# Two heads' low parts of P in one GpSimd operation, and another table for the sums ahead of the main loop

## The chip, the cores and the metric

The kernel runs on one core of a Trainium2 chip. The metric is the time in microseconds that the device takes for one launch; smaller is better. The kernel before takes 1578.27 us, the median of three runs (1576.91 to 1578.88).

## What is computed

Attention over a band of 256 keys and a bilinear feed-forward network share one normalised input; the network's output gates the attention's.

```
H = 32; Dh = D // H; W = 256                      # B, S, D, F = 1, 2048, 576, 4608
xn = layernorm(x)
q, k, v = split(xn @ wqkv)                         # per head, 18 wide
scores = einsum("bhqd,bhkd->bhqk", q, k) * Dh**-0.5
p = softmax(where(0 <= q_index - k_index < W, scores, -1e9))
s = (p @ v) @ wo
g = silu(((xn @ w_gate) * (xn @ w_up)) @ w_down)
out = x + s * g
```

## The kernel before

Every matrix product works on 16-bit floats, and each operand is split in two parts, a high and a low one (the value rounded to 16 bits, and what the rounding left), so that a product is hi*hi + hi*lo + lo*hi.

The program has a prologue and a main loop. The prologue (lines 660 to 855) normalises x into `XT`, projects V, Q and K, and writes them to memory in the device. The main loop (lines 1287 to 1291) has 72 slots of 16 places: slot `sl` is the feed-forward network's step for group `g = sl // 4` of 256 hidden columns and chunk `c = sl % 4` of 512 rows. TensorE's work of a place is issued by `seven_place` (lines 1150 to 1180), a fast matrix product with seven products of blocks instead of eight. It needs sums of blocks of x (`SX`, from `s_steps`, lines 525 to 592, made once for each chunk) and of the weights (`TW`, from `t_sum`, `t_hi`, `t_lo`, lines 494 to 519, made anew for each group). `seven_read` reads the products out of the PSUM banks named `up`, of which there are two: a product that writes into a bank waits until ScalarE (`seven_copy`, L1126) or VectorE (`seven_add`, L1130) has read it. `seven_mult` (L1135) multiplies, once on GpSimd (`ht`) and once on VectorE (in place in `gt`). `h_hi` (L1002, ScalarE) and `h_lo` (L1008, VectorE) split the result into `hh`, and `down` (L1024) multiplies it by the third weight.

Everything else hangs on a list of times: `at(slot, place, f, ...)` queues a call, `at_place` issues the calls of a place, and the dict `AT` holds the numbers. The engines run their own instructions strictly in the order in which these calls issue them, so that AT is the order of the work on each engine.

Attention has 64 steps, one in each of the slots 1 to 64. A step `s` takes a pair of heads `j = 0, 1` for four blocks `i = 0..3` of 128 queries. For each of the eight (i, j) five calls follow one another at places of the table "p": `score` (L908, VectorE, writes the masked scores to a tile `sm_` and their maximum), `shifted` (L916), `probs` (L920, the exponential on ScalarE; with j = 1 also L923, which rounds both heads' P to the high parts in the tile `pp`), `turn_probs` (L929, the low parts: P minus its high part, into the same `pp`; with j = 1 also L932, the transposing DMA from `pp` to `pt`) and `weigh` (L941, the product with V). Both heads of an i share one tile `sm_` of 2 x 384 floats, and there are two such tiles (line 905), so block i + 2 writes where block i was read. The steps 0 to 15 have shorter rows (128, 256, 384, 384 keys for i = 0..3); later ones have 384 each.

The line that decides who makes the low parts is L929 in `turn_probs`: `AT["en"][(s + 1) % 4][2 + 2 * i + j]` is 0 for GpSimd and 1 for VectorE. All four rows of "en" are (0, 1, 0, 0, 0, 0, 1, 0, 0, 0): for i = 0, 1, 3 both heads are GpSimd's, for i = 2 the first head is VectorE's and the second GpSimd's.

The prologue's part of the order is in the entries "sx" (time of each of the 17 steps of `s_steps` for each chunk), "on" (which of these are VectorE's, 1, or GpSimd's, 0), and "g0", "t0", "u0", "wd0" (group 0's weights).

Of the kernel before, what the change touches and what calls it, by code (L numbers as in the profile page):

```python
# [13 lines left out]
OP = mybir.AluOpType  # L14
# [6 lines left out]
def kernel(  # L21
# [10 lines left out]
    nc = tc.nc  # L32
# [6 lines left out]
    NCH = S // 512  # L39
# [28 lines left out]
    AT = {"amax": (19, 20, 6),  # L68
           "dn": ((41, 45), (51, 52), (52, 48)),
           "down": ((6, 9, 12, 15, 20), (6, 8, 11, 14, 16), (6, 8, 11, 14, 16), (6, 9, 12, 15, 19)),  # L70
           "en": ((0, 1, 0, 0, 0, 0, 1, 0, 0, 0), (0, 1, 0, 0, 0, 0, 1, 0, 0, 0),
                  (0, 1, 0, 0, 0, 0, 1, 0, 0, 0), (0, 1, 0, 0, 0, 0, 1, 0, 0, 0)),
           "end": ((30, 32, 35), (28, 32, 33), (28, 32, 33), (28, 32, 33)),
           "eng": (1, 1, 0, 1, 1, 0, 1, 0, 0, 0, 0, 0, 0, 1),
           "g0": (-22, -19, -22, -21, -9, -16, -14, -11, -11),
           "h": (((15, 17), (18, 21)), ((15, 17), (19, 21)), ((15, 17), (21, 21)), ((15, 17), (19, 21))),
           "load": (8, 3, 15),
           "mult": {1: 6, 4: 18, 5: 1, 6: 0},
# [13 lines left out]
           "raw": (8, 9, 12, 16, -6, 0),  # L92
           "scale": (26, 28, 35, 51),
           "sum": ((30, 36, 50, 59, 64), (41, 53, 56, 61, 62)),
# [5 lines left out]
           "t_hi": ((57, 57), (67, 69)),  # L100
           "t_lo": ((57, 58), (70, 71)),
           "u0": ((-9, -8, -7, -7), (-7, -7, -7, -4)),
           "up_hi": (36, 36, 60, 61),
           "up_lo": (41, 40, 65, 62),
           "wd": ((55, 56), (65, 69), (70, 74)),
           "wd0": ((-4, 3), (-1, 4), (-1, 7))}

    ctx.enter_context(tc.manual_schedule())
    const = ctx.enter_context(tc.tile_pool(name="const", bufs=1))
# [573 lines left out]
    a, b = TB.pop(0)  # L683
# [96 lines left out]
    for t in range(16):  # L780
# [18 lines left out]
        elif t in (3, 5):  # L799

            k = (t + 5) // 2 - 1
# [54 lines left out]
    post = ctx.enter_context(tc.tile_pool(name="post", bufs=1, reuse_waits="tile"))  # L856
    acc = post.tile([128, NT, D], F32, name="acc")
    att = att_stack.enter_context(tc.tile_pool(name="att", bufs=1))
    QS, KS, VT, SP, SM, PP, PT, PVB, OB, O3, MX, SMT, RC = {}, {}, {}, {}, {}, {}, {}, {}, {}, {}, {}, {}, {}

    def unit(u, part, n0, n1):
        return qk_d[part:part + 3, u * DH:(u + 1) * DH, n0:n1]
# [55 lines left out]
    def probs(s, j, i):  # L918
        sm, mx, n = SM[s, j, i]
        nc.scalar.activation(sm, sm, AF.Exp, bias=mx[:, 1:2], scale=sig[:, 0:1])  # L920
        if j == 1:
            PP[s, i] = att.tile([128, 1536], F16, name="pp", bufs=3)
            nc.scalar.copy(PP[s, i][:, 0:2 * n].rearrange("p (j n) -> p j n", j=2), SMT.pop((s, i))[:, :, 384 - n:])  # L923


    def turn_probs(s, j, i):
        sm, mx, n = SM.pop((s, j, i))
        pp, a = PP[s, i], n * j
        (nc.gpsimd, nc.vector)[AT["en"][(s + 1) % NCH][2 + 2 * i + j]].tensor_tensor(pp[:, a + 2 * n:a + 3 * n], sm, pp[:, a:a + n], op=OP.subtract)  # L929
        if j == 1:  # L930
            pt = PT[s, i] = att.tile([128, 12, 128], F16, name="pt", bufs=3)
            nc.sync.dma_start(pt[:, 0:4 * n // 128], PP.pop((s, i))[:, 0:4 * n], transpose=True)  # L932
# [51 lines left out]
    for s in range(NSTEP):  # L984
        b = first_slot + s
        for f, p in zip((load_k, load_q, load_v), AT["load"]):
            at(b - 1, p, f, s)
        for k in range(2):
            at(b, AT["pairs"][k], score_pairs, s, 2 * k)
        for n in range(8):  # L990
            i, j = divmod(n, 2)
            for f, p in zip((score, shifted, probs, turn_probs, weigh), AT["p"][b % NCH][n]):
                at(b, p, f, s, j, i)
        at(b, AT["end"][b % NCH][0], finish, s)
        at(b, AT["end"][b % NCH][1], finish2, s)
        if s % 2 == 1:
            for part in range(3 if s % 16 == 15 else 2):
                at(b, AT["end"][b % NCH][2] + 2 * part, store_o, s // 16, s % 16 // 2, part)
# [327 lines left out]
```

## Time and profile before

| | |
|---|---|
| runs | 1578.27 us median (1576.91 to 1578.88) |
| the profiled execution | 1577.54 us, span 1575.8 us |
| TensorE busy | 1555.8 us, 99% |
| VectorE busy | 1268.4 us, 80% |
| ScalarE busy | 1069.8 us, 68% |
| GpSimd busy | 850.8 us, 54%, 1066 instructions |
| granted TensorE clock | 1.0 of full speed throughout |

The span is the time from the first to the last instruction of the profiled execution; the execution's own time is 1.7 us longer. Busy is the time in which an engine executes something, waits in an instruction that has begun included.

### The profile page before, as it was taken

Reading aid. Unit: us, or ns where it says so; the run is one execution under the profiler, and the core shown is the slowest. Engines: PE = TensorE matmul, PEld = TensorE weight load, DVE = VectorE, ACT = ScalarE, POOL = GpSimd, SP = SyncE. Lnnn points to the kernel's source line nnn. Section 1 sums busy time; section 2 is a strip of 40 time slices with the busy share of each in tenths; the row PEclk is TensorE's granted clock in tenths of the full one; section 3 lists DMA queues with packets and bytes.
Section 4 is the critical chain, followed back from the end, with each engine's and each line's share of the span. In section 5 each row is a group of like instructions: output and inputs, shape, how many; then the busy total and the mean of one; then the engine's idle time right before and its main releaser. Section 6 shows DMA issues by size and latency. Waiting matters only on the chain.

```text
span 1575.8 us, 40062 instructions
## 1 busy us (share of the span) xinstructions
PE 1555.8 (99%) x15498; PEld 1106.1 (70%) x15498; DVE 1268.4 (80%) x2756; ACT 1069.8 (68%) x1854; POOL 850.8 (54%) x1066
## 2 busy tenths in 40 slices
PE   8999999999999999999999999999999999999999
PEld 5465577777777777777777777777777777777767
DVE  6537688888888988898989888888888888877654
ACT  6535477777777878777778777878778787752230
POOL 4116455656465757575766666566757575742100
PEclk9999999999999999999999999999999999999999
DMA  8683436555557676777777677767696877651338
GB/s 221 200 249 129 164 73 135 100 127 108 121 107 139 126 148 127 144 139 139 139 129 156 119 148 125 155 119 150 118 154 128 152 124 148 120 103 33 68 83 219
DMA packets 566575, 212.14 MB, mean 135 GB/s; under 512 B 504560, under 2 KB 544624, under 8 KB 566384
## 3 DMA queue, kind: packets, MB, share of 16 engines
q1 hardware_dynamic: 566384, 209.58, 64.3%
q8 instruction: 121, 1.98, 0.6%
q14 instruction: 70, 0.57, 0.1%
HBM read 76.63 MB, written 29.00 MB: 67 GB/s over the span
## 4 chain that ended last, share of the span: by engine, by line
PE 86%; DVE 6%; POOL 2%; DMA 2%; issue 1%; ACT 1%; SPq 0%; DVEq 0%; POOLq 0%; ACTq 0%
PE up L1160 41%; PE dn L1024 22%; PE pv L941 4%; PE s L387 4%; PE up L1113 3%; PE s L897 2%; PE s L1024 2%; PE s L1263 2%; PE up L1263 2%; PE up L387 1%; DVE hh L1008 1%; DMA pt<-pp 1%; PE s L338 1%; POOL pp L929 1%; DVE tw L193 1%
## 5 line engine op out<-in xcount | busy, mean ns | idle before, releaser
L1024 PE MATMUL dn<-dnw,hh 128*128 128x512 f16 (+1 forms) x3168 | 444.7, 286 | 1.1
L1160 PEld LDWEIGHTS <-tw 128*128 128x128 f16 x3456 | 319.2, 97 | 63.5 <-DVE tw L193 6.0
L1024 PEld LDWEIGHTS <-hh 128*128 128x128 f16 x3456 | 222.4, 98 | 169.2 <-issue 19.2
L1160 PEld LDWEIGHTS <-upw 128*128 128x128 f16 x3024 | 283.9, 98 | 64.5 <-issue 22.2
L1130 DVE SCALAR_TENSOR_TENSOR gt<-up,gt 128x512 f32<-128x512 f32 x360 | 247.6, 688 | 60.7 <-PE up L1113 40.1
L1031 DVE SCALAR_TENSOR_TENSOR acc<-dn,sc,acc 128x512 f32<-128x512 f32 x310 | 215.2, 694 | 99.1 <-PE dn L1024 99.1
L1160 PE MATMUL up<-XT,upw 128*128 128x256 f16 x2160 | 276.6, 273 | 0.0
L916 ACT ACTIVATE mx<-mx,sig 128x2 f32<-128x2 f32 x256 | 98.0, 383 | 212.7 <-DVE mx L908 212.7
L1160 PE MATMUL up<-XT,tw 128*128 128x256 f16 x1728 | 234.8, 272 | 3.4 <-DVE gt L1130 3.4
L1160 PE MATMUL up<-sx,tw 128*128 128x256 f16 x1728 | 224.7, 272 | 2.6 <-DVE tw L193 2.5
L1135 POOL TENSOR_TENSOR ht<-gt 128x512 f32<-128x512 f32 x72 | 92.1, 1279 | 93.1 <-DVE gt L1130 92.3
L941 PEld LDWEIGHTS <-pt 128*128 128x128 f16 x2880 | 109.7, 96 | 38.1 <-DMA pt<-pp 3.0
L941 PE MATMUL pv<-vt,pt 128*128 128x37 f16 x2880 | 112.9, 179 | 1.9 <-DMA pt<-pp 1.9
L1160 PE MATMUL up<-sx,upw 128*128 128x256 f16 x864 | 112.7, 273 | 0.0
L1126 ACT ACTIVATE gt<-up 128x512 f32<-128x512 f32 x144 | 83.6, 581 | 30.8 <-PE up L1160 17.3
L1002 ACT ACTIVATE hh<-ht 128x512 f16<-128x512 f32 x72 | 45.2, 627 | 67.4 <-POOL ht L1135 67.4
L507 POOL TENSOR_TENSOR tf<-raw 128x256 f32<-128x256 f32 x102 | 83.5, 818 | 0.1
L507 POOL TENSOR_TENSOR tf<-raw,tf 128x256 f32<-128x256 f32 x68 | 62.0, 913 | 21.7 <-DVE tw L193 21.7
L193 DVE SCALAR_TENSOR_TENSOR upw<-raw,sc,upw 128x640 f16<-128x640 f32 x72 | 71.7, 998 | 0.0
L315 ACT ACTIVATE upw<-raw 128x1280 bf16<-128x1280 f32 (+1 forms) x51 | 62.5, 1226 | 5.9 <-DMA raw<-in_B_w_up_dram 5.6
L193 DVE SCALAR_TENSOR_TENSOR tw<-tf,sc,tw 128x512 f16<-128x512 f32 x68 | 49.4, 749 | 14.5 <-ACT tw L190 13.7
L897 PE MATMUL s<-ks,qs 54*128 54x384 f16 (+2 forms) x512 | 60.2, 312 | 0.0
(1355 smaller groups left out, 2921.8 us busy)
## 6 DMA issues: line engine op xcount, KB each, us to landing
raw<-in_B_w_down_dram SPq DMA_DIRECT2D x36, 288.0 KB
qk_d<-qp SPq DMA_DIRECT2D x18, 512.0 KB
raw<-in_B_w_gate_dram SPq DMA_DIRECT2D x36, 256.0 KB
raw<-in_B_w_up_dram SPq DMA_DIRECT2D x36, 256.0 KB
ks<-qk_d SPq DMA_DIRECT2D x96, 81.0 KB
qs<-qk_d SPq DMA_DIRECT2D x128, 54.0 KB
vt<-v_d SPq DMA_DIRECT2D x48, 111.0 KB
qk_d<-qp SPq DMA_DIRECT2D x20, 256.0 KB
```

Of the source, the lines that this page charges most:

```text
L193: nc.vector.scalar_tensor_tensor(w, rv, s, h, op0=OP.mult, op1=OP.subtract)
L387: nc.tensor.matmul(ps, a, b, start=i == 0 and not opened, stop=i == 12 and opened)
L507: nc.gpsimd.tensor_tensor(t[:, to], x0, x1, op=OP.subtract)
L897: nc.tensor.matmul(ps[:, :hi_ - lo_], QS[s][r, i * 128:(i + 1) * 128], KS[s][r, lo_:hi_], start=True, stop=True)
L916: nc.scalar.activation(mx[:, 1], mx[:, 0], AF.Identity, bias=sig[:, 2:3], scale=sig[:, 1:2])
L941: nc.tensor.matmul(PVB[s][:, j, i, :VW], pt[:, nb * j + n + n // nb * nb], VT[s][:, lo_ + n % nb, j * VW:(j + 1) * VW], start=n == 0, stop ...
L1024: nc.tensor.matmul(to, a, b, start=q == 0, stop=q == len(l) - 1)
L1031: nc.vector.scalar_tensor_tensor(d, src, SC[g][:, 9:10], d, op0=OP.mult, op1=OP.add)
L1126: nc.scalar.activation(seven_new(sl, name), CH[q], AF.Copy, scale=H_SC)
L1130: nc.vector.scalar_tensor_tensor(seven_new(sl, name), CH[q], H_SC, x, op0=OP.mult, op1=OP.add)
L1135: eng.tensor_tensor(HT[sl, f], u[:, 0], u[:, 1], op=OP.mult)
L1160: nc.tensor.matmul(CH[q][:, o], a, b, start=CH["first"], stop=last and q not in (1, 2, 5), skip_group_check=q in ON)
```

## The change

`turn_probs` no longer issues two operations where both heads of a block are GpSimd's: the call with j = 0 issues nothing, and the call with j = 1 issues one operation over both heads (2 x n elements in a row, read from the whole tile `sm_`, which `probs` now keeps in `BOTH`). Where the heads are shared between the engines (i = 2) nothing changes. The lines after the function move down by eight.

```diff
         if j == 1:
             PP[s, i] = att.tile([128, 1536], F16, name="pp", bufs=3)
-            nc.scalar.copy(PP[s, i][:, 0:2 * n].rearrange("p (j n) -> p j n", j=2), SMT.pop((s, i))[:, :, 384 - n:])
+            nc.scalar.copy(PP[s, i][:, 0:2 * n].rearrange("p (j n) -> p j n", j=2), SMT[s, i][:, :, 384 - n:])
+            BOTH[s, i] = SMT.pop((s, i))
...
     def turn_probs(s, j, i):
         sm, mx, n = SM.pop((s, j, i))
         pp, a = PP[s, i], n * j
-        (nc.gpsimd, nc.vector)[AT["en"][(s + 1) % NCH][2 + 2 * i + j]].tensor_tensor(pp[:, a + 2 * n:a + 3 * n], sm, pp[:, a:a + n], op=OP.subtract)
+        on = AT["en"][(s + 1) % NCH][2 + 2 * i:4 + 2 * i]
+        e = (nc.gpsimd, nc.vector)[on[j]]
+        if on[0] != on[1]:
+            e.tensor_tensor(pp[:, a + 2 * n:a + 3 * n], sm, pp[:, a:a + n], op=OP.subtract)
+        elif j == 1:
+            h, l = (pp[:, 2 * n * k:2 * n * k + 2 * n].rearrange("p (j n) -> p j n", j=2) for k in range(2))
+            e.tensor_tensor(l, BOTH.pop((s, i))[:, :, 384 - n:], h, op=OP.subtract)
```

The table changes in the entries that set the prologue's order; the ones of the main loop ("p", "dn", "h", "sum", "t_hi" and so on) stay. Of it only two lines:

```diff
-           "g0": (-22, -19, -22, -21, -9, -16, -14, -11, -11),
+           "g0": (-22, -22, -20, -23, -10, -15, -14, -11, -11),
...
-           "wd0": ((-4, 3), (-1, 4), (-1, 7))}
+           "wd0": ((-4, 0), (-1, 6), (-1, 7))}
```

TensorE's order and that of the DMA queue (SP) stay as they were, instruction by instruction. GpSimd loses 192 of its 448 operations of L929, and one operation of the sums goes from it to VectorE.

GpSimd's order in the last of a group's four slots (c = 3), in the middle of the main loop, before. `sm__17215` holds block i = 0 of this step and `sm__17230` block 1, `sm__17362` block 2, `sm__17366` block 3; `tf` are sums of weights for the next group:

```order
L507 TENSOR_TENSOR tf<-raw_16348 128x256
L929 TENSOR_TENSOR pp<-sm__17215,pp 128x384
L507 TENSOR_TENSOR tf<-raw_16264,tf 128x256
L929 TENSOR_TENSOR pp<-sm__17215,pp 128x384
L929 TENSOR_TENSOR pp<-sm__17230,pp 128x384 x2
L507 TENSOR_TENSOR tf<-raw_16348,tf 128x256
L507 TENSOR_TENSOR tf<-raw_16348 128x256
L1135 TENSOR_TENSOR ht<-gt_17113 128x512
```

and with the change, in the same slot (tiles are numbered anew):

```order
L507 TENSOR_TENSOR tf<-raw_16218 128x256
L507 TENSOR_TENSOR tf<-raw_16135,tf 128x256
L937 TENSOR_TENSOR pp<-sm__17077,pp 128x768
L937 TENSOR_TENSOR pp<-sm__17092,pp 128x768
L507 TENSOR_TENSOR tf<-raw_16218,tf 128x256
L507 TENSOR_TENSOR tf<-raw_16218 128x256
L1143 TENSOR_TENSOR ht<-gt_16976 128x512
```

Block 0's first head stood ahead of a sum of weights and now stands behind it, in one operation with the second head. In the three other slots of a group the two heads' operations stood next to each other and only become one.

VectorE's order at the start of the main loop, around the end of slot 0, before (L1130 are reads of `up`, L547, L551, L560, L563 steps of the sums of x, L1008 the low parts of `hh`):

```order
L1130 SCALAR_TENSOR_TENSOR gt_1907<-up,gt_1907 128x512
L1130 SCALAR_TENSOR_TENSOR gt_1962<-up,gt_1962 128x512
L551 TENSOR_TENSOR XT<-tf,XT 128x2x256
L1135 TENSOR_TENSOR gt_1962<-gt_1962 128x2x256
L551 TENSOR_TENSOR sx_1804<-tf,sx_1804 128x512
L560 TENSOR_TENSOR tf<-XT_84 64x256
L560 TENSOR_TENSOR tf<-XT 64x256
L563 TENSOR_TENSOR tf<-tf 64x256
L1008 SCALAR_TENSOR_TENSOR hh<-hh,ht 128x512
L1008 SCALAR_TENSOR_TENSOR hh<-hh,gt_1962 128x512
```

and with the change:

```order
L1138 SCALAR_TENSOR_TENSOR gt_1908<-up,gt_1908 128x512
L547 TENSOR_TENSOR tf<-tf,XT 128x512
L1138 SCALAR_TENSOR_TENSOR gt_1960<-up,gt_1960 128x512
L551 TENSOR_TENSOR XT<-tf,XT 128x2x256
L1143 TENSOR_TENSOR gt_1960<-gt_1960 128x2x256
L551 TENSOR_TENSOR sx_1845<-tf,sx_1845 128x512
L560 TENSOR_TENSOR tf<-XT_84 64x256
L560 TENSOR_TENSOR tf<-XT 64x256
L1016 SCALAR_TENSOR_TENSOR hh<-hh,ht 128x512
L1016 SCALAR_TENSOR_TENSOR hh<-hh,gt_1960 128x512
```

One step of the sums (L547) came over from GpSimd, and another (L563) went behind the low parts of `hh`.

## Rows read from the trace of the kernel before

**Rows 1.** Windows: stretch, us; busy PE, PEld, DVE, ACT, POOL; clock, DMA share, GB/s

```profile
180.00:202.00 22.00, 18.91 (x166) 14.89 (x166) 20.20 (x36) 14.66 (x26) 6.28 (x5) 1.00 0.47 148
202.00:540.00 338.00, 338.00 (x3554) 248.29 (x3553) 286.48 (x671) 254.64 (x464) 203.35 (x276) 1.00 0.57 115
540.00:1400.00 860.00, 854.39 (x9285) 621.33 (x9284) 745.93 (x1631) 675.56 (x1139) 553.92 (x669) 1.00 0.74 138
```

**Rows 2.** Waits, whole span: waiter, releaser, us in total, times, longest

```profile
PEld L1024 <- DVE hh L1008: 10.8, 25, 0.7
PEld L1160 <- DVE tw L193: 6.0, 13, 0.7
PE pv L941 <- DMA pt<-pp: 1.9, 3, 1.1
```

**Rows 3.** Timeline of PE, 1074 to 1082 us: start, us, what, idle before

```profile
1074.52 1.75 PE L1024 MATMUL dn<-dnw,hh 128*128 128x512 f16 x6
...
1078.30 1.46 PE L1024 MATMUL dn<-dnw,hh 128*128 128x512 f16 x6
1079.60 0.60 PE L1160 MATMUL up<-sx,tw 128*128 128x256 f16 x4
1080.04 0.46 PE L941 MATMUL pv<-vt,pt 128*128 128x37 f16 x12
1080.34 0.38 PE L1160 MATMUL up<-sx,tw 128*128 128x256 f16 x2
1081.02 0.61 PE L1160 MATMUL up<-sx,tw 128*128 128x256 f16 x4 [0.30 <-DVE tw L193]
```

**Rows 4.** Timeline of POOL in that slot, 1061 to 1075 us

```profile
1061.83 0.92 POOL L929 TENSOR_TENSOR pp<-sm__17215,pp 128x384 f16<-128x384 f32 x1 [2.00 <-ACT pp L923]
1063.52 1.17 POOL L507 TENSOR_TENSOR tf<-raw,tf 128x256 f32<-128x256 f32 x1 [0.77 <-DVE tw L193]
1064.65 0.92 POOL L929 TENSOR_TENSOR pp<-sm__17215,pp 128x384 f16<-128x384 f32 x1
1065.53 1.80 POOL L929 TENSOR_TENSOR pp<-sm__17230,pp 128x384 f16<-128x384 f32 x2
1067.27 0.73 POOL L507 TENSOR_TENSOR tf<-raw,tf 128x256 f32<-128x256 f32 x1
...
1073.39 1.23 POOL L929 TENSOR_TENSOR pp<-sm__17362,pp 128x384 f16<-128x384 f32 x1
```

**Rows 5.** Timeline of DVE from that slot on, 1067 to 1083 us

```profile
1067.36 0.56 DVE L908 CUSTOM_DVE_ANT_0 sm__17366<-s,bias 128x384 f32<-128x384 f32 x1
...
1072.33 0.48 DVE L1031 SCALAR_TENSOR_TENSOR acc<-dn,sc,acc 128x256 f32<-128x256 f32 x1 [0.27 <-PE dn L1024]
...
1073.78 1.40 DVE L1008 SCALAR_TENSOR_TENSOR hh<-hh,ht 128x512 f16<-128x512 f16 x1
1075.10 0.68 DVE L1008 SCALAR_TENSOR_TENSOR hh<-hh,gt 128x512 f16<-128x512 f16 x1
...
1078.21 0.35 DVE L193 SCALAR_TENSOR_TENSOR wd<-raw,sc,wd 64x128 f16<-64x128 f32 x1
...
1082.26 1.10 DVE L193 SCALAR_TENSOR_TENSOR wd<-raw,sc,wd 64x128 f16<-64x128 f32 x1
```

**Rows 6.** Line 929: forms of one operation, ns min/median/max, first and last start

```profile
L929 POOL TENSOR_TENSOR pp<-sm__2148,pp x2: 428/430/431, 205.1 to 205.5; 128x128 f16<-128x128 f32 x2
L929 POOL TENSOR_TENSOR pp<-sm__2264,pp x2: 917/917/917, 216.6 to 217.5; 128x384 f16<-128x384 f32 x2
```

**Rows 7.** Timelines of DVE and PE in the last slot of an early group

```profile
470.64 0.68 DVE L1008 SCALAR_TENSOR_TENSOR hh<-hh,gt 128x512 f16<-128x512 f16 x1
...
471.16 1.47 PE L1024 MATMUL dn<-dnw,hh 128*128 128x512 f16 x6
```

**Rows 8.** Timeline of PE at the start of the main loop

```profile
186.87 1.47 PE L1160 MATMUL up<-XT,tw 128*128 128x256 f16 x12 [2.11 <-DVE gt L1130]
...
200.55 1.14 PE L1160 MATMUL up<-XT,tw 128*128 128x256 f16 x9 [0.28 <-DVE gt L1130]
```

More of the change, by code (lines that the diff above doesn't have):

```diff
@@ L94 @@
            "sum": ((30, 36, 50, 59, 64), (41, 53, 56, 61, 62)),
[5 rows of a table removed]
[5 rows of a table added]
            "t_hi": ((57, 57), (67, 69)),
            "t_lo": ((57, 58), (70, 71)),
-           "u0": ((-9, -8, -7, -7), (-7, -7, -7, -4)),
+           "u0": ((-9, -8, -7, -7), (-7, -7, -7, -1)),
            "up_hi": (36, 36, 60, 61),
@@ L858 @@
     att = att_stack.enter_context(tc.tile_pool(name="att", bufs=1))
-    QS, KS, VT, SP, SM, PP, PT, PVB, OB, O3, MX, SMT, RC = {}, {}, {}, {}, {}, {}, {}, {}, {}, {}, {}, {}, {}
+    QS, KS, VT, SP, SM, PP, PT, PVB, OB, O3, MX, SMT, RC, BOTH = {}, {}, {}, {}, {}, {}, {}, {}, {}, {}, {}, {}, {}, {}
     def unit(u, part, n0, n1):
```

18 rows, old and new, of the table AT are left out of this document.

## Prediction

> **What bounds the kernel now.** I read the windows first, to see where TensorE ever stands still. It is the engine that sets the end: between 202 and 540 us it is busy for 338.00 of 338 us, between 540 and 1400 us for 854.39 of 860, in the first slot and its approach (180 to 202 us) for 18.91 of 22 [rows 1]. GpSimd, which loses most of the work here, is busy for 553.92 of the 860 us: shortening its sum alone buys nothing. Only what it does to TensorE's few waits counts, so the second view is the list of waits. Two recur in the main loop: weight loads of L1024 wait for VectorE's `hh` (25 times), and those of L1160 for VectorE's `tw` (13 times); a third, for the transposed P, comes three times [rows 2].
>
> The third view is the timeline of one such place. Six products of L1024 usually take 1.46 us and here 1.75: 0.29 us lost on `hh`. Four products of L1160 start 0.44 us apart in sum (1079.60 to 1080.04), two therefore 0.22; the two that start at 1080.34 should be followed at 1080.56, and the next starts at 1081.02: 0.46 us lost on `tw` [rows 3]. That is 0.75 us, once in each group of four slots. The 25 waits on `hh` are two for each of twelve groups and one at the end; the groups lie between 540 and 1400 us. So some 9 us of stall are there to win or to enlarge: TensorE's modelled ends hide part of it, and the window shows only 5.6 us of it as idle [rows 1].
>
> The fourth view says why, on the two engines behind it, in the same slot. GpSimd ends the operations on block 1 at 1067.33 (1065.53 + 1.80) [rows 4], and VectorE's score operation for block 3, which writes into block 1's tile, starts at 1067.36 [rows 5]: GpSimd's chain releases VectorE there with nothing to spare. From there to the late `hh` VectorE is idle for only 0.27 us that I can name, at 1072.33 [rows 5].
>
> **The change, part by part.**
>
> *One operation for two.* An operation takes 430 ns over 128 columns and 917 over 384 [rows 6]: 1.90 ns a column. For 768 columns that makes 0.917 + 384 x 0.00190 = 1.65 us. Two of 384 start 0.88 apart and occupy GpSimd for 1.74 us up to the next operation's start (1065.53 to 1067.27), the 917 ns being 0.04 longer than the distance [rows 4]; the merged one so takes 1.61 and saves 0.13. A bound on the other side: nothing saved, 1.74. Times 192 that is 25 us of GpSimd's work. In the three slots of a group in which the pair stood together, TensorE has no wait that this shortens: worth nothing to the end, the cover being TensorE's own work.
>
> *The moved half.* In the last slot the pair of block 0 was split by a sum of weights. Its first half ran from 1061.83 in time that was free: GpSimd then stood idle for 0.77 us until VectorE let go of `tf` [rows 4]. Now that half runs behind the sum. The sum's start hangs on VectorE, not on GpSimd, so it stays at 1063.52. The merged operation on block 0 goes from 1064.65 to 1066.26, that on block 1 from 1066.26 to 1067.87, where the next sum started at 1067.27: **0.60 us later**, and with no saving in the operations 0.86 later. The change thus lengthens the one stretch of GpSimd that is waited for, while it shortens all others.
>
> *What waits for it.* VectorE's score operation of block 3 moves from 1067.36 by the same 0.60, and all of VectorE behind it in order: weights' low parts, the sum into `acc`, both operations of `hh`, then `tw`. Of the shift the 0.27 us idle at 1072.33 [rows 5] absorb some: 0.33 us are left. Then comes the meeting with GpSimd's operation on block 2, 1073.39 to 1074.62 [rows 4]: the first `hh` operation takes 1.40 us, the second 0.68 [rows 5], 0.72 lost by waiting. With both engines later by unequal amounts the collision can vanish (0.33 - 0.72 = -0.39), stay as it is (0.33), or hit the second operation as well (0.33 + 0.72 = 1.05, and 1.32 if the 0.27 aren't absorbed). I take 0.33 and a third of 0.72, **0.55 us a group**: GpSimd's row there stays dense, so that one collision remains and a second is less likely than not. TensorE's wait for `hh` and then for `tw` grows by that much. Twelve groups: 6.6 us.
>
> *Early groups.* In the steps with shorter rows the second `hh` operation ends at 471.32; its user, the last of six products that start at 471.16, comes 5/6 of 1.47 us in, at 472.4 [rows 7]: 1.1 us of slack. The moved half is one of 128 columns there, 0.43 us less 0.13 [rows 6]. It is covered: 0.
>
> *The table.* TensorE's and SP's order don't change, and TensorE's first waits of the main loop, for a read of `up`, lose 2.11 and 0.28 us [rows 8]. The operations of VectorE ahead of the first are the same ones in the same order, so I leave the 2.11. Near the other, one operation of the sums has come in (bounds 0 to 0.7 us) and one has gone behind `hh` (0.42); I take 0, with -0.7 and +0.7 as ends, and with all 3.1 us of idle of that window [rows 1] as the most that a table could ever give.
>
> **Sum.** The profiled execution took 1577.54 us; 6.6 more make 1584.1. The median of the runs lies 0.7 above that execution, so **1584.9 us**. A measurement of this kernel can tell about 0.2%, 3.2 us, from no change.
>
> **A rule against the change.** The first `hh` operation took 1.40 us where its sister took 0.68, and ended just after GpSimd's operation on block 2 [rows 4, 5]: VectorE stood still while GpSimd read. The Trainium skill (SBUF, "Who interferes with whom") has a rule that fits: a VectorE instruction with two inputs in SBUF and a GpSimd instruction that reads SBUF share an interface, and the second to start waits until the first is through. The trace agrees, with 0.72 us. By that rule the merged operation holds VectorE off for up to 1.61 us instead of 0.88 before letting it in between; that is the rival C below.
>
> **The rivals.**
>
> A, *faster*: the shift moves the two engines past each other. It decides if VectorE's `hh` operations fall between GpSimd's, so that 0.72 us are saved against 0.33 lost: -0.39 a group, 12 x 0.39 = 4.7, 1573.6 us; with all of the 0.75 gone it would be 9 us, 1569. For it: 25 us less work on GpSimd, and that one collision feeds both waits. Against it: the rows behind 1064.65 leave GpSimd no gap into which VectorE could slip.
>
> B, *no change*: VectorE's idle time takes up the whole shift, or the new place of the collision costs nothing. 1578.3 us, give or take 3. For it: 0.27 us are there to absorb, and the ends of my 0.55 lie on both sides of zero. Against it: the 0.03 us between 1067.33 and 1067.36.
>
> C, *slower by the longer hold*: in the next slot VectorE's low part of `wd` takes 1.10 us where it otherwise takes 0.35 [rows 5], which I put down to the first half of that slot's pair for block 0. Held to the end of the merged one it loses 1.61 - 0.88 = 0.73 more. If VectorE has no slack there, that comes on top, 12 x 0.73 = 8.8: 1593.7 us. Against it: no wait of TensorE is seen just behind that place.
>
> D, *slower by the transposes*: block 2's operation on GpSimd (1073.39) feeds a transposing DMA for which TensorE already waits in three groups, up to 1.1 us [rows 2]. If it moves by 0.60 + 0.4 and not VectorE's chain but this one ends last, a group loses 1 us: 12 us, 1590.3.
>
> **How the numbers follow.** The forecast 0.45 (it holds from 1581.5 to 1588), D 0.09, C 0.07, B 0.22, A 0.17. Slower by over 0.2% are the forecast, C and D: 0.61. Same is B, 0.22; faster is A, 0.17. The range from 1573 to 1593 takes in the forecast, B and D whole and the half of A that keeps one of the two stalls; C and the rest of A are out, some 0.15. It also takes in the bounds a group, -0.39 to 1.32 us (1573.6 to 1594.1), but for its last microsecond.
>
> **What would show it.** Right: between 540 and 1400 us GpSimd's busy time falls by some 18 us while TensorE's group grows by half a microsecond; in the last slot of a group the merged operation on block 0 starts behind the sum, block 1's ends some 0.6 us later against TensorE's work, and VectorE's score of block 3 starts right behind it; the waits for `hh` and `tw` have grown. Step by step wrong: a merged operation that takes far from 1.65 us; a score operation of block 3 that doesn't wait for GpSimd; an `hh` operation without a collision, which would make A of it. The whole is wrong if the time falls by over 3.2 us, or if it grows while the groups between 540 and 1400 us stay as long as they were, since then the table did it.

## The result, and the profile after

The changed kernel takes 1583.67 us, the median of six runs (1582.35 to 1585.36), where the kernel before took 1577.83 beside it (1576.51 to 1579.64): 1.0036 times as long, with an interval of 1.0027 to 1.0046. It is slower by 5.8 us. The profiled execution took 1584.01 us, span 1582.3.

Windows of the changed kernel (columns as in [rows 1]):

```profile
187.00:190.60 3.60, 3.60 (x21) 2.59 (x19) 3.15 (x6) 1.92 (x4) 1.25 (x1) 0.55 0.28 70
202.00:540.00 338.00, 338.00 (x3555) 248.30 (x3554) 288.02 (x671) 254.99 (x465) 192.12 (x219) 1.00 0.58 114
540.00:1400.00 860.00, 849.72 (x9197) 616.74 (x9195) 755.72 (x1627) 669.10 (x1130) 527.77 (x532) 1.00 0.73 137
```

Between 540 and 1400 us GpSimd does its work in 26 us less, TensorE is idle for 10.3 us where it was idle for 5.6, and VectorE is busy for 10 us longer without having more to do: busy time contains what an instruction waits after it has begun [rows 1]. Between 202 and 540 us TensorE is busy throughout, as before.

Waits of the changed kernel (as in [rows 2]):

```profile
PEld L1032 <- DVE hh L1016: 14.6, 26, 0.9
PE dn L1032 <- DVE hh L1016: 5.0, 12, 0.4
PEld L1168 <- DVE tw L193: 4.1, 8, 0.5
PE pv L949 <- DMA pt<-pp: 3.4, 4, 1.0
```

The wait for `hh` has grown and now stops the products themselves too, once in each of twelve groups; the one for `tw` did not grow. The transposed P came late four times where it was three [rows 2].

TensorE's timeline, first before, then changed: the start of the six products that wait for `hh` (L1024 before, L1032 now) in two groups that follow each other, one wait for `tw`, and places in the slot shown before:

```profile
847.66 1.75 PE L1024 MATMUL dn<-dnw,hh 128*128 128x512 f16 x6
...
923.24 1.67 PE L1024 MATMUL dn<-dnw,hh 128*128 128x512 f16 x6
...
1067.41 1.46 PE L1024 MATMUL dn<-dnw,hh 128*128 128x512 f16 x6
```

```profile
849.98 1.25 PE L1032 MATMUL dn<-dnw,hh 128*128 128x512 f16 x5
...
856.87 0.61 PE L1168 MATMUL up<-sx,tw 128*128 128x256 f16 x4 [0.26 <-DVE tw L193]
...
926.02 1.25 PE L1032 MATMUL dn<-dnw,hh 128*128 128x512 f16 x5
...
1071.22 1.46 PE L1032 MATMUL dn<-dnw,hh 128*128 128x512 f16 x6
...
1080.09 0.39 PE L1032 MATMUL dn<-dnw,hh 128*128 128x512 f16 x1 [0.41 <-DVE hh L1016]
...
1085.31 0.47 PE L949 MATMUL pv<-vt,pt 128*128 128x37 f16 x12 [0.77 <-DMA pt<-pp]
```

A group took 923.24 - 847.66 = 75.58 us and takes 76.04. The sixth product now stands behind a gap that is recorded as idle; the groups in which `pt` is late as well are longer still.

GpSimd's timeline in that slot, changed (for [rows 4]):

```profile
1067.34 1.18 POOL L507 TENSOR_TENSOR tf<-raw,tf 128x256 f32<-128x256 f32 x1 [3.71 <-DVE tw L193]
1068.48 1.65 POOL L937 TENSOR_TENSOR pp<-sm__17077,pp 128x768 f16<-128x768 f32 x1
1070.08 1.66 POOL L937 TENSOR_TENSOR pp<-sm__17092,pp 128x768 f16<-128x768 f32 x1
...
1077.12 1.04 POOL L507 TENSOR_TENSOR tf<-raw 128x256 f32<-128x256 f32 x1
1078.12 1.36 POOL L934 TENSOR_TENSOR pp<-sm__17222,pp 128x384 f16<-128x384 f32 x1
...
1086.15 1.65 POOL L937 TENSOR_TENSOR pp<-sm__17416,pp 128x768 f16<-128x768 f32 x1 [3.43 <-ACT pp L923]
```

VectorE's timeline there (for [rows 5]):

```profile
1066.51 1.41 DVE L193 SCALAR_TENSOR_TENSOR tw<-tf,sc,tw 128x512 f16<-128x512 f32 x2 [1.14 <-ACT tw L190]
...
1071.77 0.56 DVE L908 CUSTOM_DVE_ANT_0 sm__17226<-s,bias 128x384 f32<-128x384 f32 x1 [0.56 <-POOL pp L937]
...
1076.39 0.47 DVE L1039 SCALAR_TENSOR_TENSOR acc<-dn,sc,acc 128x256 f32<-128x256 f32 x1
1076.79 0.79 DVE L934 TENSOR_TENSOR pp<-sm__17222,pp 128x384 f16<-128x384 f32 x1
1077.50 1.21 DVE L1016 SCALAR_TENSOR_TENSOR hh<-hh,ht 128x512 f16<-128x512 f16 x1
1078.64 1.40 DVE L1016 SCALAR_TENSOR_TENSOR hh<-hh,gt 128x512 f16<-128x512 f16 x1
...
1086.56 1.39 DVE L193 SCALAR_TENSOR_TENSOR wd<-raw,sc,wd 64x128 f16<-64x128 f32 x1
```

GpSimd's time free of work now lies ahead of the sum (3.71 us idle), and both merged operations behind it. VectorE's score of block 3 stands for 0.56 us before GpSimd lets go of the tile; the idle 0.27 us ahead of `acc` are gone; and both `hh` operations are held while GpSimd works, the first by 0.53 us beside a sum of weights and the second by 0.72 beside the operation on block 2, over the 0.68 that one takes; before, only the first was [rows 5].

### The profile page after: what moved, and what is told of

The parts are those of the page before. It is cut to its first block, busy times and chain, and to the rows that moved or that the text cites. A ratio compares the mean times of both kernels' runs of the same rounds, so it can differ in the third digit from the quotient of the medians.

```text
span 1582.3 us, 39633 instructions
## 1 busy us (share of the span) xinstructions
PE 1559.6 (99%) x15498; PEld 1107.4 (70%) x15498; DVE 1284.4 (81%) x2757; ACT 1069.5 (68%) x1854; POOL 814.6 (51%) x873
## 4 chain that ended last, share of the span: by engine, by line
PE 68%; DVE 11%; POOL 6%; issue 5%; ACT 5%; DMA 2%; SPq 0%; DVEq 0%; ACTq 0%; POOLq 0%
PE up L1168 31%; PE dn L1032 16%; PE s L387 4%; POOL pp L937 3%; PE pv L949 2%; PE s L1032 2%; PE up L1121 2%; POOL tf L507 2%; DVE acc L1039 2%; PE s L1271 2%; PE s L897 2%; DVE gt L1138 2%; PE up L1271 2%; PE up L387 1%; DMA pt<-pp 1%
## 5 line engine op out<-in xcount | busy, mean ns | idle before, releaser
L1032 PE MATMUL dn<-dnw,hh 128*128 128x512 f16 (+1 forms) x3168 | 444.6, 286 | 5.0 <-DVE hh L1016 5.0
L1032 PEld LDWEIGHTS <-hh 128*128 128x128 f16 x3456 | 223.2, 98 | 172.7 <-issue 19.2
L193 DVE SCALAR_TENSOR_TENSOR upw<-raw,sc,upw 128x640 f16<-128x640 f32 x72 | 82.4, 1147 | 0.0
```

Source lines behind the costliest of these rows:

```text
L193: nc.vector.scalar_tensor_tensor(w, rv, s, h, op0=OP.mult, op1=OP.subtract)
L1032: nc.tensor.matmul(to, a, b, start=q == 0, stop=q == len(l) - 1)
```

## The experiments

The kernel before took 1577.5 us beside the first four, some 1579 beside the others, so the ratios to it are what to compare. The merged kernels have the change's table unless it is said otherwise.

**Merged operations alone**: the change without its table.

```diff
-           "g0": (-22, -22, -20, -23, -10, -15, -14, -11, -11),
+           "g0": (-22, -19, -22, -21, -9, -16, -14, -11, -11),
...
```

> The change with the table of before, so the merged operations alone. Theory M (the moved half): in the last slot of a group block 0's first half goes behind a sum of weights, GpSimd's block 1 ends 0.6 us later, VectorE's score of block 3 waits for it; about 0.5 us a group from 540 us on, 5 to 7 us slower than before, groups 76.0 us long instead of 75.6. Rival T (the table did it): within 1.5 us of before, groups of 75.6 us.

Measured: 1584.32 us, 1.0044 [1.0032, 1.0057]. TensorE's timeline, the same place in two groups:

```profile
850.08 1.25 PE L1032 MATMUL dn<-dnw,hh 128*128 128x512 f16 x5
926.12 1.25 PE L1032 MATMUL dn<-dnw,hh 128*128 128x512 f16 x5
```

76.04 us again: the merging carries the whole loss.

**The table alone**: the kernel before with the change's table.

```diff
-           "g0": (-22, -19, -22, -21, -9, -16, -14, -11, -11),
+           "g0": (-22, -22, -20, -23, -10, -15, -14, -11, -11),
...
```

> The new table with two operations for each pair, as before. Theory M: groups of 75.6 us as before and the time within 2 us of before; at the start of the main loop the same first wait of 2.1 us, and the later one of 0.3 us gone. Rival T: 4 us or more slower than before.

Measured: 1577.41 us, 1.0000 [0.9991, 1.0009]. The later wait of 0.28 us [rows 8] is gone, as expected, but the table is worth nothing that can be told.

**The split pair kept**: all pairs are merged but the one that had a sum of weights between its halves.

```diff
-        if on[0] != on[1]:
+        if on[0] != on[1] or (i == 0 and (s + 1) % NCH == 3):
```

> The change, but in the last slot of each group block 0 keeps its two operations, one ahead of the sum of weights and one behind it; 176 of 192 merges stay. Theory M: GpSimd's block 1 ends 0.1 us earlier than before, the score of block 3 doesn't wait, groups 75.0 to 75.6 us: 0 to 7 us faster than before, most likely 1. Rival C (a merged operation holds VectorE off longer, wherever it stands): most of the loss stays, 3 us or more slower than before.

Measured: 1577.41 us, 1.0001 [0.9993, 1.0010]. 176 of the 192 merged operations are still there and the loss is gone. GpSimd's and VectorE's timelines in the slot:

```profile
1064.46 0.91 POOL L934 TENSOR_TENSOR pp<-sm__17088,pp 128x384 f16<-128x384 f32 x1
1065.34 1.64 POOL L937 TENSOR_TENSOR pp<-sm__17103,pp 128x768 f16<-128x768 f32 x1
```

```profile
1067.07 0.55 DVE L908 CUSTOM_DVE_ANT_0 sm__17238<-s,bias 128x384 f32<-128x384 f32 x1
```

Block 1 is done in time and the score waits for nothing. So it is the half that changed sides of the sum, and the merged operations in the other places cost nothing that can be told.

**The merged operation ahead of the sum**: the changed kernel with block 0's call one place earlier in a group's last slot, so that only GpSimd's order differs.

```diff
-                 ((6, 7, 8, 11, 22), (6, 7, 8, 12, 22), (7, 8, 12, 13, 22), (7, 8, 12, 13, 23),
+                 ((6, 7, 8, 11, 22), (6, 7, 8, 11, 22), (7, 8, 12, 13, 22), (7, 8, 12, 13, 23),
```

> The change, with block 0 of the last slot merged and issued one place earlier, ahead of the sum of weights, in time in which GpSimd stands idle for 1.6 us and more; GpSimd's order is all that differs. Theory M: block 1 ends 1.0 us earlier than before against TensorE's work, the waits for hh and tw shrink: 1 to 8 us faster than before, most likely 4. Rival C: slower than before by 3 us or more, as the merged operations are all there. If the position does nothing: as the change, 5.8 us slower than before.

Measured: 1581.87 us, 1.0026 [1.0015, 1.0037]: slower than before where I expected faster. TensorE's products no longer lose time on `hh`, nor the score on GpSimd, as expected, but another wait stands in their place. VectorE's, GpSimd's and TensorE's timelines:

```profile
1066.17 1.99 DVE L193 SCALAR_TENSOR_TENSOR tw<-tf,sc,tw 128x512 f16<-128x512 f32 x2 [1.15 <-ACT tw L190]
...
1071.80 2.01 DVE L193 SCALAR_TENSOR_TENSOR upw<-raw,sc,upw 128x640 f16<-128x640 f32 x1
1073.73 0.68 DVE L1138 SCALAR_TENSOR_TENSOR gt<-up,gt 128x512 f32<-128x512 f32 x1
```

```profile
1065.31 1.64 POOL L937 TENSOR_TENSOR pp<-sm__17077,pp 128x768 f16<-128x768 f32 x1 [2.02 <-ACT pp L923]
...
1071.86 1.27 POOL L1143 TENSOR_TENSOR ht<-gt 128x512 f32<-128x512 f32 x1
```

```profile
1071.00 1.46 PE L1032 MATMUL dn<-dnw,hh 128*128 128x512 f16 x6
...
1074.46 1.47 PE L1168 MATMUL up<-sx,tw 128*128 128x256 f16 x12 [0.69 <-DVE gt L1138]
```

and in the kernel before, the same operations of VectorE and GpSimd:

```profile
1067.84 0.88 DVE L193 SCALAR_TENSOR_TENSOR upw<-raw,sc,upw 128x640 f16<-128x640 f32 x1
1069.27 1.27 POOL L1135 TENSOR_TENSOR ht<-gt 128x512 f32<-128x512 f32 x1
```

I count from the six products that TensorE starts at 1067.41 before (L1024) and at 1071.00 here (L1032). GpSimd comes to `ht` 1.00 us earlier: 0.86 us behind that start, where it was 1.86. VectorE comes to the weights' low part `upw` 0.37 us later: 0.80 behind it, where it was 0.43. It comes behind two `tw` that take 1.99 us, where they take 1.41 in the changed kernel: the merged operation holds them, which is the prediction's rival C in another place. So `upw` and `ht` meet: 2.01 us for one that took 0.88. The read of `up` behind it is late, and TensorE stands 0.69 us.

**Both single operations ahead of the sum**: the kernel before with the same number changed.

```diff
-                 ((6, 7, 8, 11, 22), (6, 7, 8, 12, 22), (7, 8, 12, 13, 22), (7, 8, 12, 13, 23),
+                 ((6, 7, 8, 11, 22), (6, 7, 8, 11, 22), (7, 8, 12, 13, 22), (7, 8, 12, 13, 23),
```

> The kernel before with one number of its own table changed: in a group's last slot both operations on block 0 stand ahead of the sum of weights, and nothing is merged. It asks what slowed the merged operation in the same place (1581.87 us, 4.4 over the kernel before). Theory P (place and meeting): with GpSimd's block 1 done earlier, VectorE comes earlier to its weights' low part (upw, 128x640) and meets GpSimd's sums and ht there; that takes it from 0.88 us to 2.0, the read of up behind it is late, and TensorE loses some 0.85 us there, whatever the length of the operation on block 0. Then this kernel shows the same 2.0 us, has no wait for hh, and stands at 1579 to 1583 us. Rival H (the hold): the merged operation alone, 1.65 us long, held VectorE's tw from 1.41 to 1.99 us, and with two operations of 0.92 us VectorE gets in between; then upw doesn't meet GpSimd, the waits for hh are gone and the time is 1573 to 1577 us.

Measured: 1583.93 us, 1.0034 [1.0022, 1.0046]. VectorE's and TensorE's timelines:

```profile
1067.88 2.14 DVE L193 SCALAR_TENSOR_TENSOR tw<-tf,sc,tw 128x512 f16<-128x512 f32 x2 [1.14 <-ACT tw L190]
...
1073.66 2.00 DVE L193 SCALAR_TENSOR_TENSOR upw<-raw,sc,upw 128x640 f16<-128x640 f32 x1
```

```profile
1076.32 1.47 PE L1160 MATMUL up<-sx,tw 128*128 128x256 f16 x12 [0.69 <-DVE gt L1130]
```

The same meeting without any merged operation, so the place makes it; the time lies just above theory P's range. Of that theory's reason only half is seen: as in the last run it is GpSimd that comes earlier, and VectorE comes to `upw` 0.80 us behind the same six products (1072.86 here), later than before. Two single operations hold `tw` longer than a merged one, 2.14 us against 1.99; rival H is out.

**Ahead of the sum, and `upw` later**: the changed kernel with two numbers changed. VectorE's `upw` goes behind the read of `up` and a score.

```diff
-                 ((6, 7, 8, 11, 22), (6, 7, 8, 12, 22), (7, 8, 12, 13, 22), (7, 8, 12, 13, 23),
+                 ((6, 7, 8, 11, 22), (6, 7, 8, 11, 22), (7, 8, 12, 13, 22), (7, 8, 12, 13, 23),
...
-           "up_lo": (41, 40, 65, 62),
+           "up_lo": (41, 40, 65, 63),
```

> The changed kernel with two numbers of its table changed: the merged operation on block 0 ahead of the sum of weights, as in the run at 1581.87 us, and VectorE's last weights' low part but one (upw) in the same slot moved from in front of a read of up and a score to behind them. Theory P (the meeting of that upw with GpSimd's sums and ht costs 0.85 us a group): the read of up comes at once, TensorE's wait of 0.7 us for it goes, and the waits for hh stay away: some 75.3 us a group against 75.6 before, 1571 to 1576 us, better than both kernels. Rival H (what costs is the merged operation's hold of tw, and the late read only its follower): the read of up is still late, 1579 to 1582 us.

Measured: 1574.70 us, 0.9974 [0.9964, 0.9985], faster than both kernels. VectorE's timeline:

```profile
1068.12 0.68 DVE L1138 SCALAR_TENSOR_TENSOR gt<-up,gt 128x512 f32<-128x512 f32 x1
...
1069.96 0.92 DVE L193 SCALAR_TENSOR_TENSOR upw<-raw,sc,upw 128x640 f16<-128x640 f32 x1
```

The read of `up` no longer stands behind the meeting, and TensorE's 0.69 us are gone.

**The same two numbers without merging**: the kernel before with both edits of the last diff.

> The kernel before with the same two numbers changed and nothing merged. It tells what merging itself is worth once the order suits it: Theory P has it within 2 us of the merged kernel with the same two numbers (GpSimd's saved 36 us of busy time worth nothing to the end), 1571 to 1577 us. Rival (the hold costs in that place): it is faster than the merged one by 3 us or more. Second rival (the saved time counts): it is slower than the merged one by 3 us or more.

Measured: 1577.44 us, 0.9989 [0.9981, 0.9998]. The merged kernel was 2.7 us faster, between the bounds of theory P and the second rival. The main difference that I find in the trace is at TensorE's product behind the held `tw`:

```profile
1065.70 0.27 PE L1113 MATMUL up<-XT,upw 64*128 64x256 f16 x1 [0.20 <-DVE gt L1130]
```

In the merged kernel that product waits for nothing that is recorded as idle: the hold is 0.15 us shorter (1.99 for 2.14), twelve times, 1.8 of the 2.7 us. No run isolates the rest.

**`upw` one place later still**: the merged kernel of two numbers, with 64 in place of 63.

> As the merged kernel with the two changed numbers, with VectorE's upw one place later still, behind the multiplication in gt as well. Theory P: the read of up and the product's waits are as there; the two upw operations now follow each other behind gt, both ahead of the late operations of hh, so that their sum is unchanged: within 3 us of that run, 1571 to 1578 us. Rival: upw is wanted by TensorE early in the next group, or gt's earlier end lets a GpSimd operation meet upw there; then a new wait for upw or hh, and 1578 us or more.

Measured: 1574.38 us, 0.9972 [0.9960, 0.9983], the same as with 63.

**`upw` later alone**: the kernel before with one number changed.

```diff
-           "up_lo": (41, 40, 65, 62),
+           "up_lo": (41, 40, 65, 63),
```

> The kernel before with one number changed: VectorE's low part upw of a group's last slot behind the read of up and the score, nothing merged, block 0's two operations split by the sum of weights as they were. It asks whether the better runs (1574.4 and 1574.7 us, ratio 0.997) owe their gain to this move alone. Theory P (place and meeting; the move only repairs the meeting that the earlier block 0 made): the wait for hh stays or changes by a few tenths, 1575.5 to 1580 us, ratio 0.998 to 1.001. Rival L (the low part's place is what counts, the place of block 0 isn't): the wait for hh goes here too, 1572 to 1575 us, ratio under 0.998.

Measured: 1575.19 us, 0.9976 [0.9967, 0.9985]. Neither theory came out whole: the six products on `hh` lose 0.14 us, which is half of the 0.29 before. But against the 0.9974 and 0.9972 with block 0 ahead of the sum as well, most of the gain is the move's own. GpSimd's timeline of the kernel before (behind the sum that starts at 1067.27 [rows 4]), and of this one, with TensorE's six products in a later group:

```profile
1067.96 1.35 POOL L507 TENSOR_TENSOR tf<-raw 128x256 f32<-128x256 f32 x1
```

```profile
1066.06 0.72 POOL L507 TENSOR_TENSOR tf<-raw,tf 128x256 f32<-128x256 f32 x1
1066.74 0.73 POOL L507 TENSOR_TENSOR tf<-raw 128x256 f32<-128x256 f32 x1
...
1072.02 1.22 POOL L929 TENSOR_TENSOR pp<-sm__17362,pp 128x384 f16<-128x384 f32 x1
```

```profile
1299.55 1.60 PE L1024 MATMUL dn<-dnw,hh 128*128 128x512 f16 x6
```

The hold goes both ways: before, VectorE's `upw` stretched GpSimd's second sum from 0.73 to 1.35 us. With `upw` out of its way, GpSimd's operation on block 2 comes 5.96 us after the first of these sums (1072.02 - 1066.06) and not 6.12 [rows 4], and the first `hh` operation, which it holds, ends 0.15 us earlier against TensorE's products. Twelve groups make 1.8 us of that. The medians lie 3.8 us apart and the profiled executions 2.7: the other 0.9 of these is groups in which the transposed P was late before and is hardly late here (TensorE loses 0.4 us on it, for 1.9 [rows 2]), and no run tells whether the move does that.

**The change and `upw` later**: the changed kernel with that number alone.

> The changed kernel with that one number changed alone, the merged operation on block 0 behind the sum as the change has it. Theory P: GpSimd still ends block 1 late, VectorE's score of block 3 still waits 0.5 us for it, and hh is late: 1580 to 1586 us, ratio 1.002 to 1.005. Rival L: the meetings with GpSimd go with the low part's move and the changed kernel is as good as before or better, 1573 to 1579 us.

Measured: 1583.55 us, 1.0031 [1.0021, 1.0041]. VectorE's timeline still shows the score's wait:

```profile
1071.55 0.56 DVE L908 CUSTOM_DVE_ANT_0 sm__17226<-s,bias 128x384 f32<-128x384 f32 x1 [0.56 <-POOL pp L937]
```

So the low part's move gains nothing while the score waits. This run and the one at 1574.70 us (0.9974) differ in one thing, on which side of the sum of weights the merged operation on block 0 stands; that side is worth some 9 us here. A kernel with both single operations behind the sum was not run, so how much of this belongs to the merging itself is not shown.

**The split pair kept, and `upw` later**: both one-line edits, merged operations elsewhere.

> The changed kernel with the pair that a sum of weights splits left unmerged (1577.41 us, ratio 1.000, when that was all) and the same low part moved. In the two better runs the merged operation ahead of the sum holds VectorE's tw (1.99 us for two in place of 1.41) and TensorE loses 0.2 us on a read of up; here the hold can't be. Theory P: if the move of the low part also frees hh here, the group is 0.2 us shorter than in those runs and the time is 1571 to 1574 us; if hh stays late by 0.2 us as in the run without the move, it is 1576 to 1579. I take the second as likelier, since VectorE isn't earlier here.

Measured: 1573.87 us, 0.9966 [0.9953, 0.9980], the lowest median of all, though its interval overlaps those of the other kernels that gained. I had taken the other outcome as likelier. Its five runs (1573.11 to 1574.61) all lie below the eleven of the unmerged kernel with `upw` later, timed beside it (1574.70 to 1576.50). TensorE's six products on `hh` lose 0.07 us here (1.46 undisturbed), and 0.14 there:

```profile
1298.84 1.53 PE L1032 MATMUL dn<-dnw,hh 128*128 128x512 f16 x6
```

Block 1's pair is merged here, so GpSimd is done earlier just where `hh` waits for it: twelve times 0.07 is 0.8 of the 1.3 us between the two, and it is a place where the saving of a merged operation reaches TensorE.

**The late `tw` ahead of block 1's scores**: the merged kernel with 64, and one number more.

```diff
-           "t_lo": ((57, 58), (70, 71)),
+           "t_lo": ((57, 58), (70, 70)),
```

> As the best run so far (1574.38 us: merged, block 0 ahead of the sum, upw moved to behind gt's multiplication) with one number more: the second of VectorE's two late low parts tw in a group's first slot goes ahead of the two scores of block 1. TensorE waits there for this tw, 0.47 and 0.15 us a group. Theory: VectorE's order is all that holds it, its operands being ready; the wait goes, 12 times 0.6 us: 1567 to 1570 us. Rival: the scores are 0.67 us late, then the exponential and the transposing DMA behind them, and TensorE waits for the transposed P or for a read of up instead: 1573 us or more.

Measured: 1574.42 us, 0.9971 [0.9959, 0.9982]: nothing gained. TensorE's timeline:

```profile
1080.15 0.92 PE L1168 MATMUL up<-XT,tw 128*128 128x256 f16 x7 [0.47 <-DVE gt L1138]
```

The wait for `tw` has become one for the read of `up` that follows the scores. From the products of `sx` and `tw` behind those of the transposed P to these seven it is 1.28 us here (1080.15 - 1078.87), and 1.29 in the kernel without this number (1079.16 - 1077.87): TensorE waits there for the sum of VectorE's work, and which of these two orders it has doesn't matter.

## Why the prediction was right, step by step

- *Where it would be lost*: right. The time went into the wait for `hh` in each group between 540 and 1400 us; a group grew by 0.46 us where I had 0.55. The groups with a late `pt` make up for that: from the first such product (545.17 before, 545.20 after) to the last, eleven groups later (1377.46 and 1383.53), the kernel lost 1383.53 - 545.20 - (1377.46 - 545.17) = 6.04 us, 0.55 a group. Eleven times 0.46 is 5.1 of these; the other 1 us is late transposes, for which the forecast had nothing, so it is luck that the mean comes out at the forecast 0.55. The run that kept the split pair lost 4.5 us to late transposes in its profiled execution (1579.41 us) and nothing in its median, so they vary without the moved half. A slip in the reading: of the 25 waits for `hh` 21 lie in these groups, not 24 (9.4 of the 10.8 us).
- *One operation for two*: right, 1.65 us, starts 1.60 apart (forecast 1.61). GpSimd's busy time fell by 36 us and not 25. Two operations count 1.80 and one 1.65, which is 29 us for 192; the rest I take for shorter holds, which no run isolates. It makes no difference to the end.
- *The moved half*: right, 0.56 us of waiting at the score of block 3 for a forecast of 0.60, the sum itself as late as before. Taken back alone it removes the loss.
- *What VectorE absorbs*: right, the idle time at `acc` is gone. Counted from the six products at 1067.41 (L1024) and at 1071.22 (L1032), the score starts 0.60 us later than before, `acc` 0.25 (I had 0.33), and the second `hh` ends 0.45 later, which is the 0.46 that the group lost.
- *The meeting with GpSimd*: the size was right and the form wasn't. I gave a third of 0.72 us to a second collision. VectorE's three operations before the product are its own low part and twice `hh`. Before, the two `hh` took 1.40 and 0.68 us [rows 5], and ahead of them, on VectorE's timeline:

```profile
1072.73 1.12 DVE L929 TENSOR_TENSOR pp<-sm__17362,pp 128x384 f16<-128x384 f32 x1
```

  That is 3.20 us. They now take 0.79 + 1.21 + 1.40 = 3.40: the low part is held less, both `hh` are held, 0.20 us more in all where I had 0.24. The forecast's own sum has a slip: 0.33 and a third of 0.72 are 0.57, not 0.55, and twelve of these 6.8 us, not 6.6; it changes nothing.
- *The waits for `tw`* were to grow with `hh` and did not: where one is left TensorE stands 0.26 us for the 0.30 before [rows 3], since its own loss ahead of them gives VectorE the time, and in four groups the late transposed P comes first.
- *Early groups* and *the table*: right, zero each: 338.00 of 338 us busy as before, and 1.0000 for the table alone.
- *The rivals*: A and B are out. C's longer hold is there, `wd` takes 1.39 us for 1.10, but TensorE isn't waiting behind it, and I had priced it at 0.73 too high. I had put the 1.10 down to the first half of GpSimd's pair, but on GpSimd's timeline before the pair lasts to 1083.21:

```profile
1081.42 1.79 POOL L929 TENSOR_TENSOR pp<-sm__17557,pp 128x384 f16<-128x384 f32 x2 [3.29 <-ACT pp L923]
```

  A `wd` of 0.35 us that ends at 1083.36 starts at 1083.01, when the first half is long over, so the second half held it, which the merged operation doesn't lengthen. It takes longer now because it comes 0.41 us behind the start of GpSimd's operation and not 0.84. D isn't the main path, but adds to some groups. The Trainium skill's rule on the shared interface (SBUF, "Who interferes with whom") agrees with the meetings shown here: 2.00 us for an `upw` of 0.88.

What failed was the experiments' theories: with the merged operation ahead of the sum, and with the low part moved alone, I treated the order of one engine as the only thing that moved, and the neighbour's operations met in another place or no longer met.

## What to carry to other kernels

Before two operations of an idle-looking engine become one, look at what stood between them: the half that is moved may have run in free time and now lies on the stretch that another engine waits for, here for a tile of which there are only two. In the order that the kernel had, 36 us of saved work were worth nothing to the end, half a microsecond of one delay in each group made the kernel 5.8 us slower, and splitting that one pair got it back. In two other orders the kernel with merged operations was 1.3 and 2.7 us faster than the one without, and part of that shows at products that wait for VectorE just where GpSimd had held it or was done earlier. Where two engines hold each other, a move by one place is worth several microseconds either way, so try the neighbour's places together with it.

## What the runs showed of the chip that I had not expected

- A held operation of VectorE ended as if it had begun 0.1 to 0.2 us ahead of GpSimd's recorded end. `wd` of 0.35 us ended at 1086.56 + 1.39 = 1087.95, GpSimd's merged operation at 1086.15 + 1.65 = 1087.80; two `tw` of 1.41 us ended at 1068.16, GpSimd's at 1066.95. With `hh` in the changed kernel it is 0.12 us (1078.64 + 1.40 - 0.68 against 1078.12 + 1.36). In these three the recorded end of GpSimd's operation is later than the end of its hold; the profile's times on GpSimd are rough.
- After the same idle time of 2.1 us at the start of the main loop the granted clock fell to a mean of 0.55 of full speed between 187.0 and 190.6 us in the changed kernel's profile, mostly the lower of the two levels (1.2 GHz), and stayed at 1.00 in the profiles of the kernel before and of eight experiments. The table-only kernel, at ratio 1.0000, had it too: it belongs to the execution and explains nothing of the result. The six products of the early group [rows 7] start at 471.16 in the profile before and at 471.11 in the changed kernel's.
